# Keeping the turned w1 in DRAM between layer 1's and layer 0's backward MLP

## The chip, the cores and the metric

The kernel runs on one core of a Trainium2 chip. The metric is the device time of one execution in microseconds (us); of several runs the median counts. The core has five engines with an instruction queue each: TensorE (PE) for matrix products and transposes, VectorE (DVE), ScalarE (ACT), GpSimd (POOL) and SyncE (SP), and 16 DMA engines which move data between DRAM and the core's on-chip memory. In this kernel SyncE issues all loads and GpSimd issues all stores.

## The reference

The program computes two layers of attention over a long cache and an MLP, for one new position of two sequences, and then the gradients of the output with respect to every input but one bias.

```python
x = A_x                                        # (2, 1, 1024)
x = x + attention(layernorm(x), k_cache, v_cache, wq, wo)   # 32 query heads, 4 kv heads, 16384 keys of 128
x = x + mlp(layernorm(x), w1, b1, w2, b2)      # layernorm again, w1 (1024, 3584), gelu, w2 (3584, 1024)
x = x + attention(layernorm(x), ...)           # the same caches and weights: layer 1
x = x + mlp(layernorm(x), ...)
out_0 = x
out_1 ... out_9 = vjp(grad_out)                # A_x, k_cache, v_cache, wq, wo, w1, b1, w2, b2
```

Both layers use the same weights and the same caches. The gradients of the caches (out_2, out_3) are as large as the caches and are the sum over the two layers. All data are bf16.

## The kernel before

One pass over the program runs four phases on one core: forward layer 0 (`fwd0`), forward layer 1 (`fwd1`), backward layer 1 (`bwd1`) and backward layer 0 (`bwd0`). Between them stand the MLPs: after each `attn_fwd` the forward MLP of that layer, ahead of each `attn_bwd` the backward MLP of that layer. The place between `fwd1` and `bwd1`, where layer 1's MLP is run forward and backward, is called the turn here; the place between `bwd1` and `bwd0`, where layer 0's MLP is run backward, the middle.

The work is a list of small pieces, in the order in which they are given to `emit`; `Program.run` goes through it once, and every engine gets its instructions in that order. A piece names the chunks that it uses. A chunk is up to 1 MB of on-chip memory (128 partitions x 4096 bf16). `run` gives chunks to buffers ("slots") in the order of their first use, as early as a slot is free, and issues a chunk's load at once when it gets its slot. So the order of the loads on SyncE is the order of first use, each load waits on SyncE for the last reader of its slot, and loads run ahead of PE as far as there are slots: 14 of their own, three in the tile `last`, and two each in the tiles `e1` and `ds1` at times. From `bwd0` on six of the 14 and `last` serve other purposes. A chunk without a load (`P.chunk()`) gets a slot in the same order.

PE contracts over partitions, so for a product with a weight matrix the other way round the matrix has to be turned first, by eight 128 x 128 transposes at a time into a PSUM bank (`tp0`, `tp1`) and a copy from there by ScalarE or VectorE (`copy_bf` gives it to the less loaded one). `turned` is such a piece, which writes the turned blocks into a chunk; `w1_turned` makes the four pieces (8 + 8 + 8 + 4 transposes) that turn one of the eight chunks of w1 (128 rows x 3584). w1 is needed turned twice: by `w1_bwd(1, ...)` at the turn and by `w1_bwd(0, ...)` in the middle, and the kernel before turns it both times, from a fresh load in the middle.

At the turn the pieces for chunks 0 to 2 (`w1_now`) stand in the tail of `attn_fwd` (steps 130 to 134) and between the steps of the layernorm (`chain(lambda: mlp_in(1, xA1), ...)`), those for chunks 3 to 7 behind each chunk's forward products in `w1_fwd`. The layernorm ends in a power on GpSimd (line 463), and w1_fwd's matmuls (line 690) need its result.

In the middle the order was: the last wq products of `attn_bwd` (line 836), w1's first chunk turned as the `fill` of the layernorm's backward (`attn_in_bwd`, whose sum over partitions is the matmul of line 395), `col_to_row` for out_0 (line 418: eight fp32 transposes, two copies and the store on GpSimd), then `w2_use(i)` for the seven chunks of w2 (line 1257), with w1's chunks 1 to 5 turned between them and 6 and 7 after them, and then `w1_bwd` (line 727), behind which the turning of wo for `bwd0` begins (line 365 again).

`attn_bwd` goes through 128 steps, each with eight transposes of the V cache (line 324), their products (line 940) and, 13 steps later, the products with the K cache (line 921). `extra` hangs further pieces on steps; before, these are the last w2 products of the forward pass (`w2_last`, which finish `xM1`, the program's output, at step 118) and the turning of w2.

`PAD` sizes a tile that is never used, and so where the tiles behind it lie in memory.

Of the kernel before, what the change touches and what calls it, by code (L numbers as in the profile page):

```python
# [8 lines left out]
BF16 = mybir.dt.bfloat16  # L9
# [14 lines left out]
LAG_B = 13  # L24
LAG_K = 15
NSTG = 12
PAD = 192
STG_FROM = (0, 0, 0, 4, 8, 12)


# [23 lines left out]
class Program:  # L54
# [11 lines left out]
    def emit(self, fn, uses=()):  # L66
        i = len(self.ops)
        self.ops.append((fn, tuple(uses)))
        for c in uses:
            if c.first is None:  # L70
                c.first = i
            c.last = i
# [31 lines left out]
def kernel(  # L104
# [24 lines left out]
    nc = tc.nc  # L129
    V = nc.vector  # L130
    S = nc.scalar
    PE = nc.tensor
    GP = nc.gpsimd
# [4 lines left out]
    F = B_w1.shape[1]  # L138
    assert (B, D, HKV, SK, DH, HQ, F) == (2, 1024, 4, 16384, 128, 32, 3584)
    R = HQ // HKV  # L140
    DJ = D // 128
# [8 lines left out]
    P = Program()  # L150
    emit = P.emit
# [8 lines left out]
    small = ctx.enter_context(tc.tile_pool(name="small", bufs=3))  # L160
# [3 lines left out]
    dram = ctx.enter_context(tc.tile_pool(name="dram", bufs=1, space=bass.MemoryType.DRAM))  # L164
# [6 lines left out]
    def flat(t):  # L171
        return t.rearrange("p a b -> p (a b)")
# [5 lines left out]
    def ob():  # L178
        st["ob"] += 1
        return obanks[st["ob"] % 3]  # L180
# [29 lines left out]
    ident = const.tile([128, 128], BF16, name="ident")  # L210
    make_identity(nc, ident[:])
    identf = const.tile([128, 128], F32, name="identf")
# [11 lines left out]
    sel8 = const.tile([16, 8, 128], BF16, name="sel8")  # L224

    const.tile([128, PAD // 4], F32, name="pad")
    ident_d = dram.tile([128, 128], BF16, name="ident_d")


# [11 lines left out]
    up = [b * HKV + k for k in range(HKV) for b in range(2)]  # L241
    down = up[::-1]
# [35 lines left out]
    saved = {}  # L278
# [15 lines left out]
    def ld_rows(W, j0, rb, c0, n):  # L294

        return P.chunk(lambda ap: nc.sync.dma_start(
            ap[:, 0:rb * n].rearrange("p (j n) -> p j n", j=rb),
            W[j0 * 128:(j0 + rb) * 128, c0:c0 + n].rearrange("(j p) n -> p j n", p=128)))
# [7 lines left out]
    def ld_w1():  # L306
        return [ld_rows(B_w1, j, 1, 0, F) for j in range(DJ)]
# [4 lines left out]
    def col(c, j, n, o):  # L312
        return c.ap[:, j * n + o * 128:j * n + (o + 1) * 128]
# [19 lines left out]
    def turns_ahead(c):  # L333

        holds = [{} for _ in range(SKEW)]
        pieces = [(turn_of(lambda i=i: [c.ap[:, (i * 8 + j) * 128:(i * 8 + j + 1) * 128] for j in range(8)], h), [c])
                  for i, h in enumerate(holds)]
        return pieces, (c, holds)
# [17 lines left out]
    def turned(tiles, uses, dst, part, act=True):  # L356


        def f():
            ts = tiles()  # L360
            n = len(ts)
            st["tp"] += 1
            tp = tpb[st["tp"] % 2][:].bitcast(BF16).rearrange("p (a b) -> p a b", b=128)
            for j, t in enumerate(ts):
                PE.transpose(tp[:, j, :], t, ident[:])  # L365
            kT = dst.ap[:, part * 1024:part * 1024 + n * 128]
            if act:
                S.copy(out=kT.bitcast(I32), in_=flat(tp[:, 0:n, :]).bitcast(I32))
                load_of("act", 0.13 + 0.46 * n / 8)
            else:  # L370
                copy_bf(kT, flat(tp[:, 0:n, :]), 0.13 + 0.46 * n / 8, 0.12 + 0.57 * n / 8)
        return f, [c for c in uses if c is not dst] + [dst]
# [35 lines left out]
        emit(f, [c])  # L408

    def col_to_row(colT, dram_out):  # L410
        c = P.chunk()

        def f():
            row = c.ap[0:2, 0:D]
            for j0 in range(0, DJ, 4):
                ps = ob()[0:2, :].rearrange("p (a b) -> p a b", a=4)
                for j in range(4):
                    PE.transpose(ps[:, j, :], colT[:, j0 + j, :], identf[:])
                V.tensor_copy(out=row[:, j0 * 128:(j0 + 4) * 128], in_=flat(ps))
            GP.dma_start(dram_out, row)  # L420

        emit(f, [c])

    def chain(gen, gaps, fill=()):


        hold = {}
        fill = list(fill)

        def begin():  # L430
            hold["g"] = gen()
            next(hold["g"])

        emit(begin)
        for i in range(gaps):
            n = -(-len(fill) // (gaps - i))
            for f in fill[:n]:
                emit(*f)
            fill = fill[n:]
            emit(lambda: next(hold["g"], None))  # L440
# [242 lines left out]
    def w1_fwd(l, ws, then=lambda j: ()):  # L683

        hps = half[0, 0][:, 0:FJ * 2].rearrange("p (j b) -> p j b", b=2)
        emit(lambda: V.memset(hps, 0.0))
        for j in range(DJ):
            def f(j=j):
                for o in range(FJ):
                    PE.matmul(hps[:, o, :], lhsT=col(ws[j], 0, F, o), rhs=m_all[:, j, 2 * l:2 * l + 2],  # L690
                              start=False, stop=True, skip_group_check=True)
            emit(f, [ws[j]])
            for p in then(j):
                emit(*p)
        return hps

    def w1_turned(ws, j, dst, act=True):
        res = []
        for part, o0 in enumerate(range(0, FJ, 8)):
            n = min(8, FJ - o0)  # L700
            res.append(turned(lambda o0=o0, n=n: [col(ws[j], 0, F, o0 + o) for o in range(n)], [ws[j]], dst, part, act))
        return res

    def w2_fwd_piece(l, ws, i, fps):
        def f():
            for j in range(4):
                for o in range(DJ):
                    PE.matmul(fps[:, o, :], lhsT=col(ws[i], j, 1024, o), rhs=h_all[:, 4 * i + j, 2 * l:2 * l + 2],
                              start=False, stop=True, skip_group_check=True)
        return f, [ws[i]]  # L710
# [60 lines left out]
    def mlp_in(l, xT):  # L771
        y, rstd = yield from ln_fwd(xT[:], f"m{l}", twice=True)
        V.tensor_copy(out=m_all[:, :, 2 * l:2 * l + 2], in_=y[:])
        saved[f"m{l}"] = (y, rstd)
# [367 lines left out]
    def kept(keep, src, nm):  # L1142
        def get(g, c):
            key = (nm, g, c)
            ch = cache.pop(key, None) or ld_kv(src, g, c)
            if key in keep:
                cache[key] = ch
            return ch
        return get
# [19 lines left out]
    xM0 = vec.tile([128, DJ, 2], F32, name="xM0")  # L1169
# [8 lines left out]
    chunk_k1, chunk_v1 = kept(set(), Kv, "K"), kept(keep1, Vv, "V")  # L1178
    k_now, k_first = turns_ahead(chunk_k1(down[0], 0))
# [3 lines left out]

    ws1 = ld_w1()
    w1T = [P.chunk() for _ in range(3)] + ws1[3:]
    w1_now = [p for j in range(3) for p in w1_turned(ws1, j, w1T[j], act=False)]
    xA1 = attn_fwd(1, down, lambda: xM0, chunk_k1, chunk_v1, k_first, {130 + i: [w1_now[i]] for i in range(5)})
    chain(lambda: mlp_in(1, xA1), 2, w1_now[5:])
    hps1 = w1_fwd(1, ws1, lambda j: w1_turned(ws1, j, w1T[j], act=False) if j >= 3 else ())

    def turn_round():
        gelu_fwd(1, hps1)
# [15 lines left out]
    def chunk_v(g, c):  # L1208
        return cache.pop(("V", g, c), None) or ld_kv(Vv, g, c)

    v_now, v_first = turns_ahead(chunk_v(up[0], 0))
# [7 lines left out]
    xM1 = vec.tile([128, DJ, 2], F32, name="xM1")  # L1219
    ws2c = ld_w2()  # L1220
    extra = {}
# [15 lines left out]
    for j, s_ in enumerate(turn_steps):  # L1237
        i = j // 4
        extra.setdefault(s_, [])
        if j % 4 == 0:  # L1240
            extra[s_].append(w2_last(i))
        extra[s_].append(turned(lambda j=j, i=i: [col(ws2c[i], j % 4, 1024, o) for o in range(DJ)], [ws2c[i]],
                                ws2c[i], j % 4, act=False))
    ws1c = ld_w1()
    attn_bwd(1, up, saved["g3"], chunk_v, v_first, extra=extra, fill=w1_turned(ws1c, 0, ws1c[0]))
    col_to_row(xM1, out_0.rearrange("b s d -> (b s) d"))


    g2 = saved["gA1"]
# [2 lines left out]
    def w2_use(i):  # L1252
        def f():
            for j in range(4 * i, 4 * i + 4):
                kT = as_tiles(ws2c[i], j % 4)
                for o in range(DJ):
                    PE.matmul(dhps0[:, j, :], lhsT=kT[:, o, :], rhs=gM_all[:, o, 0:2], start=(o == 0),
                              stop=(o == DJ - 1))
        return f, [ws2c[i]]

    for i in range(FJ // 4):
        emit(*w2_use(i))
        for p in w1_turned(ws1c, i, ws1c[i], act=False) if 1 <= i < 6 else ():
            emit(*p)
    emit(lambda: V.tensor_tensor(out=dh_all[:, :, 0:2], in0=slopes[0][:], in1=dhps0, op=ALU.mult))
    for j in (6, 7):
        for p in w1_turned(ws1c, j, ws1c[j], act=False):
            emit(*p)
    dmps0 = w1_bwd(0, ws1c)
    saved["g1"] = vec.tile([128, DJ, 2], F32, name="g1")  # L1270

# [35 lines left out]
    def outputs(s, ask):  # L1307
# [6 lines left out]
        while bg and state["credit"] >= 1:  # L1314
# [3 lines left out]
        return res  # L1318

    attn_bwd(0, down, saved["g1"], chunk_v, v_first0, outputs=outputs,  # L1320
             after=lambda: col_to_row(saved["gA0"], out_1.rearrange("b s d -> (b s) d")))

    slots = [Slot(t[:], until=marks[f"bwd0 {STG_FROM[i]}"] if i < len(STG_FROM) else None) for i, t in enumerate(slot_tiles)]
    slots += [Slot(last_t[:, i * CH:(i + 1) * CH], until=marks["bwd0 0"]) for i in range(3)]
# [35 lines left out]
```

## Time and profile before

| what | value |
|---|---|
| median of 3 runs | 1188.06 us (1185.49 to 1197.34) |
| the profiled execution | 1194.48 us, its span on the core 1192.7 us |
| PE, VectorE, ScalarE, GpSimd busy | 87%, 51%, 47%, 10% of the span |
| mean granted TensorE clock | 0.864 |
| DMA | 453.83 MB, 381 GB/s over the span |
| of that loads (SyncE's queue) | 352.36 MB |
| of that stores (GpSimd's queue) | 98.66 MB |

The page and the views of the trace give the time of each instruction by line of the kernel, engine and tile. "L365 PE MATMUL tp<-ident,slot x8" is eight matmuls of line 365 (transposes are matmuls with the identity) that read a slot and write a PSUM bank. Slots carry no numbers in these names. "idle before <-X" says that the engine stood still ahead of the instruction and that X ended the wait. The granted clock is the share of full speed that TensorE had. PEld is the loading of weights into TensorE, which overlaps PE.

### The profile page before, as it was taken

The page shows a single profiled execution, that of the slowest core. Times are in us where ns is not written, and L with a number is a line of the kernel's source. Part 1 is how long each engine was busy: PE and PEld are TensorE (multiplying, and loading weights), DVE is VectorE, ACT ScalarE, POOL GpSimd, SP SyncE. Part 2 cuts the span into 40 slices and gives each one's busy share as a digit, 9 for nine tenths or more (in the row PEclk, how much of TensorE's full clock was granted, in tenths as well). Part 3 has the DMA queues.
Part 4 walks back from the last instruction along what each step waited for, and adds up shares of the span by engine and source line. Part 5 has one row for each costly group of instructions (what it writes and reads, how often), then busy time and mean ns, then how long its engine had stood idle before and what let it go on. Part 6 is the DMA issues. An engine that isn't in the chain of part 4 may idle for free. (4 is left out here: it accounts for less than half of the span.)

```text
span 1192.7 us, 44045 instructions
## 1 busy us (share of the span) xinstructions
PE 1032.3 (87%) x19762; PEld 859.1 (72%) x19805; DVE 605.4 (51%) x1266; ACT 554.8 (47%) x996; POOL 125.1 (10%) x214
## 2 busy tenths in 40 slices
PE   6878887689988988888889988988997998899996
PEld 6778786688988987888888886655565555555663
DVE  2423242224333333333434435877886787677775
ACT  2423241124333423333444424766775776567774
POOL 1000000000000000000000010322222222222222
PEclk9966695679787758889999997999998999899998
DMA  9999999989999996999999976899999999999994
GB/s 365 420 421 421 422 420 421 386 298 378 420 420 420 422 409 264 378 414 418 417 402 330 365 295 232 323 376 373 417 417 373 384 417 410 371 362 409 416 415 200
DMA packets 106041, 453.83 MB, mean 381 GB/s; under 512 B 8658, under 2 KB 8658, under 8 KB 75516
## 3 DMA queue, kind: packets, MB, share of 16 engines
q1 hardware_dynamic: 78780, 352.36, 74.5%
q0 software_dynamic: 27072, 98.66, 20.5%
q8 instruction: 154, 2.52, 0.8%
q14 instruction: 35, 0.29, 0.1%
HBM read 352.37 MB, written 98.62 MB: 378 GB/s over the span
## 5 line engine op out<-in xcount | busy, mean ns | idle before, releaser
L192 ACT COPY kT<-tp 128x512 int32<-128x512 int32 x427 | 250.0, 586 | 418.3 <-PE tp L324 391.0
L324 PE MATMUL tp<-ident,slot 128*128 128x128 bf16 x4224 | 369.2, 238 | 12.1 <-issue 5.1
L324 PEld LDWEIGHTS <-slot 128*128 128x128 bf16 x4224 | 284.4, 107 | 30.0 <-issue 12.3
L195 DVE COPY kT<-tp 128x1024 bf16<-128x1024 bf16 x209 | 144.5, 691 | 296.6 <-PE tp L324 240.8
L200 ACT CAST slot<-sc 128x512 bf16<-128x512 f32 x271 | 157.6, 589 | 50.2 <-PE sc L1072 19.6
L203 DVE CAST slot<-sc 128x512 bf16<-128x512 f32 x227 | 154.4, 688 | 38.1 <-PE sc L1025 18.6
L1025 PE MATMUL sc<-last 128*128 128x512 bf16 x324 | 119.7, 389 | 17.1 <-ACT slot L200 5.3
L921 PEld LDWEIGHTS <-slot 128*128 128x128 bf16 x1888 | 80.0, 98 | 42.5 <-issue 18.6
L940 PEld LDWEIGHTS <-kT 128*128 128x128 bf16 x2048 | 80.7, 97 | 38.5 <-issue 21.4
L1032 POOL DMA_DIRECT2D out_dram<-slot x128 | 69.0, 539 | 281.2 <-ACT slot L200 173.9
L203 DVE CAST slot<-sb 128x512 bf16<-128x512 f32 x126 | 86.7, 688 | 18.1 <-PE sb L1025 6.4
L664 PE MATMUL sc<-qd,kT 128*128 128x8 bf16 x2048 | 90.3, 171 | 2.6 <-issue 2.6
L940 PE MATMUL sc<-qd,kT 128*128 128x8 bf16 x2048 | 90.0, 170 | 1.7 <-issue 1.6
L200 ACT CAST slot<-sb 128x512 bf16<-128x512 f32 x128 | 75.3, 589 | 29.1 <-PE sb L1072 16.0
L664 PEld LDWEIGHTS <-kT 128*128 128x128 bf16 x2048 | 73.1, 99 | 3.0 <-issue 2.9
L1025 PE MATMUL sb<-last 128*128 128x512 bf16 x161 | 62.1, 386 | 6.6 <-ACT slot L200 1.6
L365 PE MATMUL tp<-ident,slot 128*128 128x128 bf16 x692 | 58.0, 239 | 6.2 <-issue 2.2
L647 PE MATMUL sb<-e,slot 128*128 128x8 bf16 x1280 | 56.7, 176 | 6.3 <-ACT e L583 3.8
L1072 PE MATMUL sc<-last 128*128 128x512 bf16 x155 | 56.6, 384 | 4.8 <-DVE last L1060 3.3
L647 PEld LDWEIGHTS <-slot 128*128 128x128 bf16 x1280 | 50.1, 102 | 9.6 <-issue 7.1
L365 PEld LDWEIGHTS <-slot 128*128 128x128 bf16 x692 | 48.2, 107 | 11.5 <-issue 9.0
L192 ACT COPY slot<-tp 128x512 int32<-128x512 int32 (+1 forms) x52 | 29.7, 574 | 52.9 <-PE tp L365 49.8
(292 smaller groups left out, 1258.7 us busy)
## 6 DMA issues: line engine op xcount, KB each, us to landing
slot<-in_A_k_cache_dram SPq DMA_DIRECT2D x101, 1024.0 KB, 10.2
slot<-in_A_v_cache_dram SPq DMA_DIRECT2D x91, 1024.0 KB, 12.1
out_dram<-slot POOLq DMA_DIRECT2D x182, 512.0 KB, 10.3
slot<-in_A_wq_dram SPq DMA_DIRECT2D x28, 1024.0 KB, 10.7
slot<-in_A_wo_dram SPq DMA_DIRECT2D x23, 1024.0 KB, 15.2
last<-in_A_v_cache_dram SPq DMA_DIRECT2D x16, 1024.0 KB, 14.4
slot<-in_B_w_dram SPq DMA_DIRECT2D x18, 896.0 KB, 13.7
slot<-in_B_w_dram SPq DMA_DIRECT2D x12, 1024.0 KB, 12.5
```

The source lines that it names most:

```text
L192: S.copy(out=dst.bitcast(I32), in_=src.bitcast(I32))
L195: V.tensor_copy(out=dst, in_=src)
L200: S.copy(out=dst, in_=src)
L203: V.tensor_copy(out=dst, in_=src)
L324: PE.transpose(tp[:, j, :], t, ident[:])
L365: PE.transpose(tp[:, j, :], t, ident[:])
L647: PE.matmul(acc, lhsT=c.ap[:, ((vi % 4) * 8 + j) * 128:((vi % 4) * 8 + j + 1) * 128], rhs=e[:, vi, :, j], start=(vi == 0 and j == 0), stop ...
L664: PE.matmul(sc[t // 64][:, :, t % 64], lhsT=kT[:, j, :], rhs=qd[:, 0, g, l, :], start=True, stop=True)
L921: PE.matmul(sb[0][:, 0:8], lhsT=c.ap[:, ((vi % 4) * 8 + j) * 128:((vi % 4) * 8 + j + 1) * 128], rhs=d[:, vi, :, j], start=(vi == 0 and j = ...
L940: PE.matmul(scb[0][t // 64][:, :, t % 64], lhsT=kT[:, j, :], rhs=qd[:, 1, g, l, :], start=True, stop=True)
L1025: PE.matmul(ps, lhsT=hold["blk"][:, 2 * (hc % 2) + u // 2, :], rhs=flat(qms[w][:, (u % 2) * 4:(u % 2) * 4 + 4, :]), start=True, stop=True)
L1032: GP.dma_start((dKv if w == 0 else dVv)[g, :, hc * 16:(hc + 1) * 16, :], stg.rearrange("p (t d) -> p t d", d=128))
```

## The change

At the turn each turned chunk of w1 is also stored into a DRAM scratch `w1_d[j]`, on GpSimd's queue (`w1_kept`). In the middle the eight chunks are loaded from there instead of from w1, and the turning of w1 in the middle goes, from the `fill` as well as from between and after `w2_use`. out_0's row is turned at step 121 of `attn_bwd(1)` instead of after it. Both output rows (out_0 and out_1) are first cast to bf16, turned by eight bf16 transposes into one bank and copied once, instead of two times four fp32 transposes and two copies. The small tile for the cast takes 32 bytes of each partition, and `PAD` shrinks by as much.

```diff
-PAD = 192
+PAD = 160
...
+    w1_d = [dram.tile([128, F], BF16, name=f"w1_d{j}") for j in range(DJ)]
     ident_d = dram.tile([128, 128], BF16, name="ident_d")
...
     def col_to_row(colT, dram_out):
+
         c = P.chunk()

         def f():
             row = c.ap[0:2, 0:D]
-            for j0 in range(0, DJ, 4):
-                ps = ob()[0:2, :].rearrange("p (a b) -> p a b", a=4)
-                for j in range(4):
-                    PE.transpose(ps[:, j, :], colT[:, j0 + j, :], identf[:])
-                V.tensor_copy(out=row[:, j0 * 128:(j0 + 4) * 128], in_=flat(ps))
+            cb = small.tile([128, DJ, 2], BF16, name="out_bf", bufs=1)
+            V.tensor_copy(out=cb[:], in_=colT[:])
+            ps = ob().bitcast(BF16)[0:2, :].rearrange("p (a b) -> p a b", a=DJ)
+            for j in range(DJ):
+                PE.transpose(ps[:, j, :], cb[:, j, :], ident[:])
+            V.tensor_copy(out=row, in_=flat(ps))
             GP.dma_start(dram_out, row)

-        emit(f, [c])
+        return f, [c]
...
+    def w1_kept(ws, j, dst):
+
+        return w1_turned(ws, j, dst, act=False) + [(lambda: GP.dma_start(w1_d[j][:], dst.ap[:, 0:F]), [dst])]
...
-    w1_now = [p for j in range(3) for p in w1_turned(ws1, j, w1T[j], act=False)]
-    xA1 = attn_fwd(1, down, lambda: xM0, chunk_k1, chunk_v1, k_first, {130 + i: [w1_now[i]] for i in range(5)})
-    chain(lambda: mlp_in(1, xA1), 2, w1_now[5:])
-    hps1 = w1_fwd(1, ws1, lambda j: w1_turned(ws1, j, w1T[j], act=False) if j >= 3 else ())
+    w1_now = [p for j in range(3) for p in w1_kept(ws1, j, w1T[j])]
+    w1_tail = {130: w1_now[0:1], 131: w1_now[1:2], 132: w1_now[2:3], 133: w1_now[3:5], 134: w1_now[5:6]}
+    xA1 = attn_fwd(1, down, lambda: xM0, chunk_k1, chunk_v1, k_first, w1_tail)
+    chain(lambda: mlp_in(1, xA1), 2, w1_now[6:])
+    hps1 = w1_fwd(1, ws1, lambda j: w1_kept(ws1, j, w1T[j]) if j >= 3 else ())
...
-    ws1c = ld_w1()
-    attn_bwd(1, up, saved["g3"], chunk_v, v_first, extra=extra, fill=w1_turned(ws1c, 0, ws1c[0]))
-    col_to_row(xM1, out_0.rearrange("b s d -> (b s) d"))
+    extra.setdefault(121, []).append(col_to_row(xM1, out_0.rearrange("b s d -> (b s) d")))
+    ws1c = [P.chunk(lambda ap, j=j: nc.sync.dma_start(ap[:, 0:F], w1_d[j][:])) for j in range(DJ)]
+    attn_bwd(1, up, saved["g3"], chunk_v, v_first, extra=extra)
...
     for i in range(FJ // 4):
         emit(*w2_use(i))
-        for p in w1_turned(ws1c, i, ws1c[i], act=False) if 1 <= i < 6 else ():
-            emit(*p)
     emit(lambda: V.tensor_tensor(out=dh_all[:, :, 0:2], in0=slopes[0][:], in1=dhps0, op=ALU.mult))
-    for j in (6, 7):
-        for p in w1_turned(ws1c, j, ws1c[j], act=False):
-            emit(*p)
     dmps0 = w1_bwd(0, ws1c)
...
-             after=lambda: col_to_row(saved["gA0"], out_1.rearrange("b s d -> (b s) d")))
+             after=lambda: emit(*col_to_row(saved["gA0"], out_1.rearrange("b s d -> (b s) d"))))
```

## The prediction

> **What bounds the kernel now.** I read the page's head first, then busy time by stage, then the waits, then the two places that the change touches in order of time.
>
> The page's head, with the busy share of the DMA engines in 40 slices:
>
> ```profile
> span 1192.7 us, 44045 instructions
> ...
> DMA  9999999989999996999999976899999999999994
> ```
>
> The DMA engines look like the bound, with holes only at the layer-1 turn (slice 15) and between the two backward passes. The windows by stage say which engine sets the pace in each; columns are window and length, busy time of PE, its weight loads, VectorE, ScalarE and GpSimd, granted clock, DMA share and GB/s.
>
> ```profile
> core 0: us, PE busy (x) PEld busy (x) DVE busy (x) ACT busy (x) POOL busy (x), PEclk, DMA share, GB/s
> 425.00:450.00 25.00, 21.39 (x464) 19.84 (x462) 7.16 (x23) 6.28 (x13) 0.69 (x1) 0.62 1.02 406
> 450.00:465.00 15.00, 12.98 (x322) 12.04 (x321) 6.56 (x21) 6.32 (x12) 0.00 (x0) 0.98 0.30 111
> 465.00:490.00 25.00, 21.10 (x422) 20.56 (x420) 8.86 (x34) 7.03 (x13) 0.00 (x0) 0.67 1.01 419
> 510.00:610.00 100.00, 84.76 (x2069) 83.31 (x2069) 38.56 (x94) 38.63 (x66) 0.00 (x0) 0.91 1.02 419
> 610.00:682.00 72.00, 67.53 (x1725) 65.13 (x1726) 30.02 (x67) 31.31 (x54) 0.00 (x0) 1.00 0.95 354
> 682.00:715.30 33.30, 29.59 (x683) 27.53 (x681) 11.82 (x29) 9.33 (x17) 4.54 (x3) 0.87 0.80 307
> 740.00:830.00 90.00, 80.31 (x1061) 51.58 (x1061) 71.38 (x122) 64.06 (x119) 25.42 (x42) 0.98 0.93 351
> 830.00:1170.00 340.00, 308.73 (x4296) 200.53 (x4319) 261.13 (x457) 234.76 (x430) 84.78 (x147) 0.96 1.00 397
> ```
>
> At the turn (450 to 465) the engines move 111 GB/s against 419 when full, so some 308 x 15 = 4.6 MB of room lies unused there. From 610 on the rate is below full and PE is busy 89 to 94% of each stage: PE's order is the pace.
>
> Who waits for loads. Of PE's waits from 421 us to the end, one is put to a DMA:
>
> ```profile
> PE sb L647 <- DMA last<-in_B_w_dram: 0.5, 1, 0.5
> ```
>
> SyncE, which issues the loads, from 421 to 690 us (waited for; total, times, longest):
>
> ```profile
> SPq L291 <- PE tp L324: 80.4, 26, 5.4
> ...
> SPq L291 <- PE sb L727: 20.5, 7, 18.9
> ...
> SPq L296 <- DMA out_dram<-last: 10.5, 1, 10.5
> ```
>
> PE lost 0.5 us to late data in 766 us, while SyncE waited for PE to free buffers (18.9 us in one piece for w1_bwd, L727, which is the hole). Even where DMA is full after the turn, loads run ahead of their use. A saved microsecond of PE order between 682 and 715 should therefore reach the end; added DMA bytes should not, unless they exceed the lead.
>
> **The change, part by part.**
>
> *Removed between the backward passes.* PE in order of time (start, length, line, count):
>
> ```profile
> 681.44 0.54 PE L836 MATMUL sc<-dq_all,slot 128*128 128x2 bf16 x16
> ...
> 684.36 0.53 PE L395 MATMUL sb<-lb_s,onesf 128*128 128x4 f32 x2
> 684.75 1.76 PE L418 MATMUL sc<-identf,xM 128*2 128x128 f32 x8
> 686.40 1.75 PE L1257 MATMUL sc<-gM_all,slot 128*128 128x2 bf16 x64
> ...
> 708.66 0.85 PE L727 MATMUL sb<-dh_all,last 128*128 128x2 bf16 x28
> ...
> 715.25 3.60 PE L365 MATMUL tp<-ident,slot 128*128 128x128 bf16 x32
> ```
>
> ```profile
> 681.00:709.00 28.00, 17.24 (x224) 14.68 (x224) 0.88 0.78 303
> ```
>
> The second fence is line 365 alone: the 224 transposes that turn w1 hold PE for 17.24 us, and PE's waits for their evictions lie between them. They go, with 32 copies on ScalarE and VectorE, and so do the eight float transposes of L418; the layernorm's matmul (L395) even stood behind the first 28 of them. What they covered comes into the open. The old stretch ran from 681.98 (end of L836) to 715.25, 33.3 us. The new one has four links. First, the layernorm's chain. The same chain stands uncovered at the end of the program:
>
> ```profile
> 1170.38 0.34 PE L836 MATMUL sb<-dq_all,slot 128*128 128x2 bf16 x8
> ...
> 1173.27 1.01 PE L418 MATMUL sc<-identf,gA 128*2 128x128 f32 x4 [1.30 <-DVE gA L968]
> ...
> 1174.08 1.06 PE L418 MATMUL sb<-identf,gA 128*2 128x128 f32 x4
> ...
> 1176.85 1.01 PE L1057 MATMUL sc<-ident,dq_all 128*4 128x128 bf16 x8
> 1177.97 0.70 DVE L1060 COPY last<-sc 4x1024 bf16<-4x1024 bf16 x1 [0.75 <-PE sc L1057]
> ```
>
> From 1170.72 to 1173.27 is 2.55 us; with one more cast, 2.8. Second and fourth, w2_use and w1_bwd, 224 two-column matmuls each, now back to back. Their rate, from L727 alone (busy PE, count, PE's weight loads, clock):
>
> ```profile
> 462.00:464.40 2.40, 2.40 (x96) 2.40 (x96) 1.00 0.25 51
> 464.90:468.00 3.10, 3.08 (x116) 2.99 (x113) 0.50 1.03 425
> ```
>
> That is 25 ns at full clock and 26.6 ns at half, so a clock that falls here costs little; 224 x 26 = 5.8, twice. Third, the slope product on VectorE, formerly behind the last transposes: about 0.5 us by the links of the chain above. Sum 2.8 + 5.8 + 0.5 + 5.8 = 14.9; saved 33.3 - 14.9 = 18.4, call it 18.2. Bounds: nothing, if read-back data come too late (a rival), to 33.3 - 11.6 = 21.7 with both chains covered.
>
> *The read-back* loads the same 8 x 896 KB in SyncE's old places, but SyncE now reaches them differently. out_0's row, formerly stored after the pass, takes a buffer from the K loads at about 641 us and holds it to its store, now at step 121, near 662. One K load then waits for that store, and the eight w1 loads queue behind it. The old issues in SyncE's order of time, and the row's store from its issue to landing (shortest, median, longest of two):
>
> ```profile
> 659.22 2.98 SPq L291 DMA_DIRECT2D slot<-in_A_k_cache_dram  x2
> 666.11 0.33 SPq L296 DMA_DIRECT2D last<-in_B_w_dram  x1
> 669.97 11.51 SPq L296 DMA_DIRECT2D slot<-in_B_w_dram  x7
> ```
>
> ```profile
> DMA to landing us min/median/max: 1.6/3.3/5.1
> ```
>
> ```profile
> 678.76 1.20 PE L921 MATMUL sb<-ds,slot 128*128 128x8 bf16 x40
> ```
>
> Transposed near 662.5, copied 0.7, the row is issued at 664 and lands by 669; the K load follows at 669 instead of 662. The last 32 of those 40 matmuls at 679 are its first use. At 419 GB/s it and the eight w1 loads (8.4 MB) are through 20 us later, about 691 to 693 with latency. w1_bwd, from 691.1, needs the last chunk near 696, and the two wo loads behind it (2.5 us each) meet their first uses 2 to 3 us early. I take no wait, with a bound of 7 us for the K load's whole delay.
>
> *The row itself* at step 121 sits in PE's order inside the PE-bound stage: eight bf16 transposes (1.01 us for eight at the reduced clock, above; half of that at full) and a wait for the cast: +0.7. At the end, two fp32 groups (1173.27 to 1175.14, 1.87 us) become a cast plus eight bf16 transposes, about 1.3: -0.6.
>
> *Added at the turn.* Eight stores of 128 x 3584 bf16, 7.34 MB, on GpSimd's queue. Two of them, j = 1 and 2, stand ahead of the layernorm's power on that queue, for which VectorE, and after it PE's first w1_fwd matmul, wait:
>
> ```profile
> 439.41 0.43 DVE L195 COPY slot<-tp 128x512 bf16<-128x512 bf16 x1 [0.47 <-PE tp L365]
> ...
> 439.98 0.69 POOL L463 TENSOR_TENSOR m_rstd<-ln_vpe,neghalf 128x2 f32<-128x2 f32 x1 [177.76 <-DVE ln_vpe L460]
> ...
> 441.25 0.89 PE L690 MATMUL sc<-m_all,slot 128*128 128x2 bf16 x28 [1.71 <-DVE sc L686]
> ```
>
> ```profile
> L1032 POOL DMA_DIRECT2D out_dram<-slot x128: 531/532/570, 740.5 to 1183.6; - x128
> ...
> DMA to landing us min/median/max: 2.9/10.3/18.0
> ```
>
> The last copy of j = 2 ends at 439.84; an issue of 0.53 us follows, so the power starts about 0.5 late: +0.5 (0.5 to 1.5, if seven-KB rows issue slower). The other six stores have nothing behind them on GpSimd until out_0. The seven loads that take w1's buffers after w1_bwd (462 to 468) now also wait for landings; issued from about 427 to 456 for the first seven, the stores land by 466 at the median, 474 at the longest.
>
> The bytes: 7.34 MB less the 4.6 MB of the hole is 2.7 MB, 6.5 us of lag for loads issued after 463. Taken as nothing: the DMA engines already stood nearly still for longer than that (450 to 465) and PE met no late load afterwards. If that cover were gone, the price is 7.34 / 0.419 = 17.5 us. Those are the bounds, 0 and 17.5.
>
> The Trainium skill, "DMA: Bandwidth & Descriptors", section "Queues, rings and completion order", says each DMA engine takes turns between its queues packet by packet, so a store would take half the rate from the w1 loads that w1_fwd wants next. No run here shows two queues at the turn yet. By that page's fabric ceiling (435 GB/s, "Specifications") the stores would cost an estimated 16.9 us if nothing hid them.
>
> *Sum:* -18.2 + 0.7 - 0.6 + 0.5 = -17.6 us. On the profiled execution's own 1194.48 us that is 1176.9; it ran 6.4 above the median of the runs shown, 1188.06, which becomes **1170.5**. The last stage keeps its own order, buffers and load distance, so I let it start earlier as a whole.
>
> **Rivals.**
>
> *A, stores paid in full.* The eight stores delay the w1 loads, and through them the turn's chain, by their whole 17.5 us; the middle still gains. 1188.1 - 17.6 + 17.5 = 1188. For it: 406 GB/s at 425 to 450, already full. Against: the hole, and PE's single DMA wait.
>
> *B, the read-back is late.* SyncE stands at the K load until out_0's row has landed; w1, wo and v come 7 us late in a stage where I counted 2 to 3 us of room, then another 2 or so behind a fuller queue. The gain falls by about 7: 1177.5. For it: SyncE already lost 10.5 us to this row. Against: its landing takes at most 5.1.
>
> *C, slower: bytes are the bound.* The last pass runs at DMA share 1.00 for 340 us. If it ends when its bytes are through rather than when PE is, an earlier start gives nothing, and the stores' 17.5 us are added: 1205.6. It decides from the point where PE begins to wait for loads or its staging for stores. For it: that share. Against: 397 GB/s there and 351 before it, against 419; PE busy 91%.
>
> **How the numbers follow.** Forecast 0.64, A 0.16, B 0.12, C 0.08. From 1164, nearly the largest saving of the middle (21.7) and the sum's smaller terms with a little run-to-run spread, to 1189, which takes in A and B; C lies outside. A measurement of this kernel can tell about 1% from no change: 11.9 us. The forecast and a small part of B lie beyond: faster 0.65; most of B and A are the same, 0.24; C and a piece of A slower, 0.11.
>
> **What would show it.** Right: line 365 absent between the passes, w1_bwd ending 14 to 16 us after the last wq matmul, a second DMA queue with 7.3 MB filling the hole, no new PE wait on loads. A: w1_fwd of layer 1 waiting for DMA and the turn longer by several microseconds. B: PE idle on DMA at w1_bwd or at the wo transposes. C: waits on out_dram growing after 830 while the last pass stretches. Wrong altogether if the stretch from L836 to w1_bwd's end stays near 33 us.

## The result, and the profile after

The changed kernel took 1184.8 us (median of 20 runs, 1179.4 to 1191.8); the kernel before, run beside it, 1195.5 (20 runs). The ratio is 0.9934, 95% interval 0.9912 to 0.9956; two later repetitions gave 0.9888 [0.9848, 0.9929] and 0.9894 [0.9858, 0.9931]. The change is faster, by about 11 us in medians and by 8 to 13 us by the three ratios, where 17.6 were forecast. The three runs of before that the prediction started from (1188.06) were quick ones, but that concerns only the absolute time, not the saving. The profiled executions went from 1194.48 to 1184.97 us, a difference of 9.5.

The head of the page after:

```profile
span 1183.2 us, 43570 instructions
## 1 busy us (share of the span) xinstructions
PE 1013.8 (86%) x19538; PEld 843.3 (71%) x19581; DVE 596.1 (50%) x1251; ACT 545.4 (46%) x979; POOL 129.8 (11%) x222
...
DMA  9999999989999999999998997899999999999994
...
q0 software_dynamic: 28224, 106.00, 22.2%
q8 instruction: 153, 2.51, 0.8%
```

The hole in slice 15 is gone, and so are 224 matmuls. Queue q0 (GpSimd's stores) carries 106.00 MB. The row that turned out to matter is the last: a queue of 153 packets of kind "instruction", 16 KB each (2.51 MB / 153).

The windows by stage after, in the columns of the prediction's:

```profile
425.00:450.00 25.00, 20.53 (x444) 19.18 (x442) 6.26 (x23) 6.09 (x12) 2.95 (x5) 0.61 1.02 416
450.00:465.00 15.00, 12.86 (x299) 11.85 (x299) 7.18 (x22) 6.40 (x13) 2.12 (x4) 1.00 1.02 418
465.00:490.00 25.00, 20.57 (x428) 20.02 (x426) 8.36 (x33) 6.27 (x11) 0.00 (x0) 0.66 1.02 425
...
652.40:686.70 34.30, 31.36 (x780) 30.03 (x776) 14.77 (x38) 14.05 (x24) 0.54 (x1) 0.95 0.92 356
686.70:689.50 2.80, 0.63 (x5) 0.56 (x4) 1.75 (x12) 0.00 (x0) 0.00 (x0) 0.54 1.05 439
689.50:698.60 9.10, 6.24 (x224) 6.10 (x224) 0.00 (x0) 0.00 (x0) 3.97 (x2) 0.50 1.02 407
698.90:707.10 8.20, 6.27 (x226) 6.19 (x226) 0.00 (x0) 0.00 (x0) 0.00 (x0) 0.50 1.04 422
```

The turn now moves 418 GB/s where it moved 111. In the middle w2_use took 9.1 us and w1_bwd 8.2, and in both PE worked for only 6.3. What it waited for in between stands in the timeline of PE (start, length, line, count; in brackets the idle time before and what ended it):

```profile
686.37 0.34 PE L844 MATMUL sb<-dq_all,slot 128*128 128x2 bf16 x8
687.37 0.59 PE L397 MATMUL sc<-lb_s,onesf 128*128 128x4 f32 x2 [0.66 <-DVE lb_s L477]
689.47 3.55 PE L1266 MATMUL sc<-gM_all,slot 128*128 128x2 bf16 x128 [1.51 <-DVE gM_all L978]
...
693.74 1.60 PE L1266 MATMUL sc<-gM_all,slot 128*128 128x2 bf16 x55
698.18 0.40 PE L1266 MATMUL sc<-gM_all,slot 128*128 128x2 bf16 x9 [2.84 <-issue]
698.88 0.88 PE L735 MATMUL sb<-dh_all,last 128*128 128x2 bf16 x28 [0.30 <-DVE dh_all L1272]
699.63 2.56 PE L735 MATMUL sb<-dh_all,slot 128*128 128x2 bf16 x91
704.12 2.21 PE L735 MATMUL sb<-dh_all,slot 128*128 128x2 bf16 x77 [1.93 <-issue]
706.20 0.89 PE L735 MATMUL sb<-dh_all,last 128*128 128x2 bf16 x28
706.94 2.64 PE L367 MATMUL tp<-ident,slot 128*128 128x128 bf16 x23
710.06 2.90 PE L367 MATMUL tp<-ident,slot 128*128 128x128 bf16 x33 [0.48 <-issue]
```

PE stops three times for "issue", that is for nothing which the profile shows: 2.84, 1.93 and 0.48 us. Count the matmuls between the stops: 9 + 28 + 91 = 128, and 77 + 28 + 23 = 128. The stops come 5.94 us apart and fall inside a chunk (119 is four chunks of 28 and seven more), so no chunk's landing ends them. The read-back was there anyway: SyncE issued its last load at 684.6, and the rows of that line say

```profile
DMA to landing us min/median/max: 7.7/9.4/10.5
```

so all of it had landed by about 695, ahead of w1_bwd's start at 698.88.

This is theory F, on which the experiments turn: PE's own instructions arrive by DMA in blocks. 19538 matmuls and 19581 weight loads are 39119 instructions; over 153 packets that is 256 per packet, so a packet holds 128 pairs of weight load and matmul. The number of packets follows that of the pairs: among the experiments below, 152 in e3, which has 112 pairs fewer, and 173 in e4, which has 2560 more (20 packets of 128). The trace's records of this queue put one packet into or just ahead of each stop: they start at 695.76, 701.77 and 707.68, last 0.9 us, and PE goes on 1.4 to 1.5 us after the end of each, at 698.18, 704.12 and 710.06. With the 16 DMA engines full, as here, a packet arrives only about every 5.9 us, 46 ns per pair. The Trainium skill ("Trainium Architecture — The Big Picture", section "The software stack") gives 64 bytes per instruction, with which 16 KB is the same 256; that section speaks of the streams being moved when the program is loaded, whereas this trace has 153 such packets within the execution.

Where the time went, in us, from one profile of before and three of the changed kernel. The pass runs from layer 1's first product on V to its last wq product, the middle from there to layer 0's first product on V; the first row includes the forward half, which scatters by some microseconds from run to run:

| stretch | before | after | repeats | difference | forecast |
|---|---|---|---|---|---|
| start to the pass | 480.54 | 481.69 | 481.94, 484.26 | +1.2, +1.4, +3.7 | +0.5 |
| the pass | 201.44 | 205.02 | 205.06, 203.69 | +3.6, +3.6, +2.3 | +0.7 |
| the middle | 54.98 | 41.76 | 41.66, 42.48 | -13.2, -13.3, -12.5 | -18.2 |
| last pass and tail | 455.75 | 454.70 | 455.68, 455.76 | -1.1, -0.1, 0.0 | -0.6 |

### The profile page after: what moved, and what is told of

Its sections match the earlier page's. It is cut to its first block, busy times and chain, and to the rows that moved or that the text cites. A ratio compares the mean times of both kernels' runs of the same rounds, so it can differ in the third digit from the quotient of the medians.

```text
span 1183.2 us, 43570 instructions
## 1 busy us (share of the span) xinstructions
PE 1013.8 (86%) x19538; PEld 843.3 (71%) x19581; DVE 596.1 (50%) x1251; ACT 545.4 (46%) x979; POOL 129.8 (11%) x222
## 3 DMA queue, kind: packets, MB, share of 16 engines
q0 software_dynamic: 28224, 106.00, 22.2%
q8 instruction: 153, 2.51, 0.8%
## 5 line engine op out<-in xcount | busy, mean ns | idle before, releaser
L326 PE MATMUL tp<-ident,slot 128*128 128x128 bf16 x4224 | 369.1, 238 | 9.9 <-issue 3.9
L326 PEld LDWEIGHTS <-slot 128*128 128x128 bf16 x4224 | 284.3, 107 | 27.5 <-issue 10.3
L200 ACT CAST slot<-sc 128x512 bf16<-128x512 f32 x263 | 153.0, 588 | 60.7 <-PE sc L1080 29.9
L203 DVE CAST slot<-sc 128x512 bf16<-128x512 f32 x242 | 163.7, 688 | 33.4 <-PE sc L1033 15.0
L1033 PE MATMUL sc<-last 128*128 128x512 bf16 x325 | 117.3, 386 | 17.5 <-DVE last L1068 5.6
L929 PEld LDWEIGHTS <-slot 128*128 128x128 bf16 x1888 | 80.6, 98 | 44.9 <-issue 20.8
L200 ACT CAST slot<-sb 128x512 bf16<-128x512 f32 x136 | 80.1, 589 | 17.7 <-PE sb L1033 9.0
L203 DVE CAST slot<-sb 128x512 bf16<-128x512 f32 x111 | 76.4, 688 | 21.2 <-PE sb L1033 8.0
L651 PEld LDWEIGHTS <-slot 128*128 128x128 bf16 x1280 | 50.3, 102 | 10.5 <-issue 6.9
L367 PE MATMUL tp<-ident,slot 128*128 128x128 bf16 x528 | 47.6, 246 | 5.4 <-issue 3.9
L929 PE MATMUL sb<-ds,slot 128*128 128x8 bf16 x864 | 41.4, 176 | 11.0 <-issue 11.0
L1033 PEld LDWEIGHTS <-last 128*128 128x128 bf16 x512 | 38.4, 98 | 16.7 <-issue 8.4
```

Of the source, the lines that this page charges most:

```text
L200: S.copy(out=dst, in_=src)
L203: V.tensor_copy(out=dst, in_=src)
L651: PE.matmul(acc, lhsT=c.ap[:, ((vi % 4) * 8 + j) * 128:((vi % 4) * 8 + j + 1) * 128], rhs=e[:, vi, :, j], start=(vi == 0 and j == 0), stop ...
L929: PE.matmul(sb[0][:, 0:8], lhsT=c.ap[:, ((vi % 4) * 8 + j) * 128:((vi % 4) * 8 + j + 1) * 128], rhs=d[:, vi, :, j], start=(vi == 0 and j = ...
L1033: PE.matmul(ps, lhsT=hold["blk"][:, 2 * (hc % 2) + u // 2, :], rhs=flat(qms[w][:, (u % 2) * 4:(u % 2) * 4 + 4, :]), start=True, stop=True)
```

## Experiments

Three theories are named in the expectations. F is the one above. S says that the missing microseconds are the price of the eight stores. D gathers the rivals in which something else sets the rate of the middle's matmuls: the arrival of the data, or the halved clock. R comes later, for the row of out_0.

### e1: the stores alone

The kernel before, with `w1_kept` at the turn and everything else as it was:

```diff
-    w1_now = [p for j in range(3) for p in w1_turned(ws1, j, w1T[j], act=False)]
+    w1_now = [p for j in range(3) for p in w1_kept(ws1, j, w1T[j])]
...
-    hps1 = w1_fwd(1, ws1, lambda j: w1_turned(ws1, j, w1T[j], act=False) if j >= 3 else ())
+    hps1 = w1_fwd(1, ws1, lambda j: w1_kept(ws1, j, w1T[j]) if j >= 3 else ())
```

> The kernel before with the eight stores of the turned w1 at the turn, and nothing else; the middle turns w1 again. Theory F (PE's instructions arrive too slowly in the middle): the stores are nearly free, layer 1's first product step of the backward pass comes 0.5 to 1.5 us later than before, and the whole is 0 to 2 us slower. Theory S (the stores' bytes or their place on GpSimd's queue eat the missing gain): 7 us or more slower than before, with waits on DMA at the turn or a bwd1 pass stretched by that much. Theory D (the read-back comes late) says the same as F here.

Measured: 1198.85 us (10 runs) against 1196.15, ratio 1.0022 [0.9988, 1.0057], so between 1.4 us gained and 6.8 lost. The windows at the turn:

```profile
450.00:465.00 15.00, 12.71 (x291) 11.59 (x289) 7.30 (x22) 6.70 (x13) 2.12 (x4) 1.00 1.03 420
```

The hole takes the stores (420 GB/s). They most likely cost about 3 us, far from the 17.5 of rival A. Layer 1's first product on V came 2.0 us later (482.53 against 480.54), a little more than the 0.5 to 1.5 expected.

### e2: the changed kernel without the stores

The read-back is replaced by loads of w1 as it stands, so layer 0's w1_bwd multiplies unturned blocks.

```diff
-        return w1_turned(ws, j, dst, act=False) + [(lambda: GP.dma_start(w1_d[j][:], dst.ap[:, 0:F]), [dst])]
+        return w1_turned(ws, j, dst, act=False) + [(lambda: None, [dst])]
...
-    ws1c = [P.chunk(lambda ap, j=j: nc.sync.dma_start(ap[:, 0:F], w1_d[j][:])) for j in range(DJ)]
+    ws1c = ld_w1()
```

> The changed kernel without the eight stores; the middle loads w1 itself, of the same bytes, and does not turn it, so its products are of the wrong matrix and only its time counts. F: the middle, from the last wq product to the end of w1_bwd, stays at 20 us (20.4 in the changed kernel), the turn gets about 1 us back, the whole is 9 to 12 us faster than before. S: the missing gain returns, 16 us or more faster than before. D: the middle stays near 20 us if late loads set it, as the loads stay.

Measured: 1186.32 us (4 runs), ratio 0.9883 [0.9824, 0.9943], an interval that takes in the changed kernel's three ratios. The middle keeps its length, 41.1 us, and its two stops (2.37 and 1.93 us). What is missing there is not the stores' price: S falls for the middle. The pass, however, took 200.9 us here against 203.7 to 205.1 with stores, though its last part, from step 112 on, was no shorter (34.5 us; 34.3 with stores). The part on the bytes at the end comes back to this.

### e3: half of layer 0's w1_bwd left out

```diff
+        no = FJ if l == 1 else FJ // 2
...
-                for o in range(FJ):
+                for o in range(no):
```

> The changed kernel with 14 instead of 28 products per chunk in layer 0's w1_bwd (half of the sum is left out); all loads stay. 112 pairs of weight load and matmul fewer. F, at 46 ns a pair: the middle falls from 20.4 us to about 15.2. By the forecast's 25 ns a pair: to 17.6. D: w1_bwd still ends with the landing of the last chunk or the wo behind it, so the start of the wo transposes moves by less than 1 us.

Measured, one run: 1178.53 us. The stretch from the last wq product to the end of w1_bwd, which the expectation calls the middle, fell from 20.4 to 15.1 us, as F had it, and so the transposes of wo start 5 us earlier, counted from that product, where D had less than 1. The whole middle up to layer 0's first product on V, however, fell only from 41.8 to 38.3 us, so there the 112 pairs were worth 3.4 us, 31 ns each. The timeline of PE shows the reason:

```profile
695.53 0.40 PE L1267 MATMUL sc<-gM_all,slot 128*128 128x2 bf16 x9 [2.66 <-issue]
696.23 0.51 PE L735 MATMUL sb<-dh_all,last 128*128 128x2 bf16 x14 [0.30 <-DVE dh_all L1273]
696.60 2.38 PE L735 MATMUL sb<-dh_all,slot 128*128 128x2 bf16 x84
698.84 0.51 PE L735 MATMUL sb<-dh_all,last 128*128 128x2 bf16 x14
699.22 0.91 PE L367 MATMUL tp<-ident,slot 128*128 128x128 bf16 x7
702.02 2.24 PE L367 MATMUL tp<-ident,slot 128*128 128x128 bf16 x19 [1.89 <-issue]
```

w1_bwd itself now runs without a stop, 3.1 us for 112, and the stop has moved into the transposes behind it, nearly as long (1.89 us) as it was. That the stop keeps its place in the instruction count (9 + 14 + 84 + 14 + 7 = 128) and not its place in the work speaks for F. So F's 46 ns are right for the stretch and too much for the whole middle, where the price lies nearer to the 25 ns of PE's own pace, probably because only part of it is held up by the blocks; one profile can't say more.

### e4: the same pairs, with quiet and with full DMA engines

Behind the end of the changed kernel stand 1536 pairs of a 128 x 128 weight load and a two-column matmul with nothing else running, then 1024 pairs while SyncE loads 32 chunks of 1 MB:

```diff
+        for n in range(1536):
+            PE.matmul(half[0, 0][:, 0:2], lhsT=t[:, 0:128], rhs=gM_all[:, 0, 0:2], start=True, stop=True)
...
+        for n in range(32):
+            nc.sync.dma_start(slot_tiles[6 + n % 8][:].rearrange("p (t d) -> p t d", d=128), Kv[n % 8, :, 0:32, :])
+        for n in range(1024):
+            PE.matmul(half[0, 0][:, 0:2], lhsT=Et[0][:, 0:128], rhs=gM_all[:, 0, 0:2], start=True, stop=True)
```

> The changed kernel with a probe behind its end, outside the reference's work: 1536 pairs of weight load and two-column matmul with no load in flight (only the last stores), then 1024 more while 32 loads of 1 MB run. F: about 26 ns a pair in the quiet part beyond the first stores (a 16-KB block of instructions every 3.4 us or faster), 46 ns a pair under load (a block every 5.9 us), so 40 and 47 us. If blocks take 5.9 us whatever the DMA engines do: 46 ns in both. If the matmuls themselves are slower in a long run (clock at half): the same figure in both, and no idle time of PE between them.

The timeline of PE, first in the quiet part, then in the loaded one:

```profile
1202.06 3.57 PE L1330 MATMUL sc<-gM_all,slot 128*128 128x2 bf16 x128 [0.17 <-issue]
1205.80 3.58 PE L1330 MATMUL sc<-gM_all,slot 128*128 128x2 bf16 x128 [0.17 <-issue]
...
1239.97 3.57 PE L1336 MATMUL sc<-gM_all,e 128*128 128x2 bf16 x128 [2.92 <-issue]
1246.18 3.57 PE L1336 MATMUL sc<-gM_all,e 128*128 128x2 bf16 x128 [2.64 <-issue]
1252.12 3.57 PE L1336 MATMUL sc<-gM_all,e 128*128 128x2 bf16 x128 [2.37 <-issue]
```

The windows of the same two parts (clock, DMA share and GB/s are the last three columns):

```profile
1180.00:1210.00 30.00, 28.43 (x1033) 27.94 (x1031) 0.00 (x0) 0.00 (x0) 0.00 (x0) 0.50 0.02 4
1222.00:1262.00 40.00, 24.34 (x877) 23.76 (x874) 0.00 (x0) 0.00 (x0) 0.00 (x0) 0.50 1.01 424
```

The groups have 128 matmuls in both parts and take 3.57 us in both. At an idle DMA the next group starts 0.17 us later (3.7 us per block, 29 ns per pair), at 424 GB/s 2.4 to 2.9 us later (5.9 to 6.2 us per block, 46 to 49 ns per pair). In all, the 1536 quiet pairs took 44.5 us, where F expected 40, and the 1024 loaded ones 46.8, where it expected 47. The records of the instruction queue show where the time goes: a packet starts 1.1 us after PE starts a block in the quiet part, but 3.6 to 3.9 us after it in the loaded part, when PE has just run dry; once started, it takes about 1 us in either. The clock is 0.50 in both, so it is not the clock, and the loaded part's operands lie still in a tile that no load writes, so it is not the data. D falls, and F is shown in isolation.

### e5 and e6: the row of out_0

The pass is 2 to 4 us longer, its last 34 us among them (31.9 before from step 112 on, 34.3 after), and SyncE's timeline after shows the wait that the prediction described:

```profile
663.98 0.33 SPq L293 DMA_DIRECT2D slot<-in_A_k_cache_dram  x1
671.48 0.33 SPq L293 DMA_DIRECT2D last<-in_A_k_cache_dram  x1
671.90 0.38 SPq L1254 DMA_DIRECT2D last<-w_d  x1
```

Theory R blames the row. e5 keeps the cast at step 121, puts the transposes into the layernorm's gap behind the pass, and takes the row's place from spare columns of two w1 chunks, so no load waits for it; e6 puts the whole row behind the pass, as before.

```diff
-    extra.setdefault(121, []).append(col_to_row(xM1, out_0.rearrange("b s d -> (b s) d")))
...
+    extra.setdefault(121, []).append((row_cast, ()))
...
-    attn_bwd(1, up, saved["g3"], chunk_v, v_first, extra=extra)
+    attn_bwd(1, up, saved["g3"], chunk_v, v_first, extra=extra, fill=[(row_store, ws1c[0:2])])
```

```diff
-    extra.setdefault(121, []).append(col_to_row(xM1, out_0.rearrange("b s d -> (b s) d")))
...
+    emit(*col_to_row(xM1, out_0.rearrange("b s d -> (b s) d")))
```

> The changed kernel again, beside the next kernels on the same chip. Both theories: ratio to the kernel before 0.990 to 0.996, middle stretch (last wq product of layer 1 to first wo product of layer 0) about 41.8 us as in its first profile.

> The cast of the first output stays at step 121, but its eight transposes run in the gap of the layernorm behind attn_bwd(1), and its store reads from columns of two w1 chunks that nothing else uses, so it holds no slot of the chunk pool and no later load waits for it. Theory R (the row, not the instruction supply, is what lengthened the end of layer 1's pass from 31.9 to 34.3 us between step 112 and its last product: SyncE's K load waited for the store): that stretch comes back to 32.0 to 32.8, and the kernel is 1.5 to 2.5 us faster than the changed kernel. Theory F (TensorE's instructions arrive 128 pairs at a time, some 46 ns a pair while the DMA engines are full, and the end of the pass runs against that): moving eight pairs wins at most 8 x 46 ns = 0.4 us and the stretch stays at 34; the difference to the changed kernel is within 0.5 us.

> The changed kernel with the first output's bf16 row put back behind attn_bwd(1), as it stood before; stores and read-back kept. Theory R: step 112 to the last product of the pass is 32.0 to 32.8 us instead of 34.3, and the row behind costs its 8 transposes and a copy on the path, about 1 us, so 0.5 to 1.5 us faster than the changed kernel. Theory F: the pass stays at about 34, and the row behind adds up to 1 us: 0 to 1 us slower than the changed kernel.

Measured: the changed kernel again 1186.21 us (the ratio is above), e5 1187.14, ratio 0.9904 [0.9869, 0.9940], e6 1189.76, ratio 0.9938 [0.9910, 0.9966]. SyncE's timeline of e5 shows that its wait is gone:

```profile
661.78 2.83 SPq L293 DMA_DIRECT2D slot<-in_A_k_cache_dram  x2
669.07 2.78 SPq L1270 DMA_DIRECT2D last<-w_d  x2
```

Yet e5's pass took 205.9 us, 34.9 of it from step 112 on: no gain, and R falls. In e6 these were 205.6 and 33.7, so the row costs the pass nothing that one profile can show, while behind the pass it lengthens the middle from 41.7 to 44.2 us. By these single profiles the move of the row is worth some 2.5 us. The medians put e6 3.5 us behind the changed kernel beside it, with intervals that overlap; R had expected it faster, F at most 1 us slower.

### e7: less read back

Only 512 of each chunk's 3584 columns are read back (the rest of what w1_bwd multiplies is what the buffer held).

```diff
-    ws1c = [P.chunk(lambda ap, j=j: nc.sync.dma_start(ap[:, 0:F], w1_d[j][:])) for j in range(DJ)]
+    ws1c = [P.chunk(lambda ap, j=j: nc.sync.dma_start(ap[:, 0:512], w1_d[j][:, 0:512])) for j in range(DJ)]
```

> The changed kernel with only 512 of the 3584 columns of each w1 chunk read back (so layer 0's w1_bwd multiplies stale columns): 6.3 MB less through the DMA engines ahead of and in the middle, the same 455 pairs on TensorE. Theory F: where the DMA share falls well below 1 in the middle, blocks of 128 pairs come 3.4 to 4.5 us apart instead of 5.9, w2_use and w1_bwd take 6 to 7 us each instead of 9.1 and 8.2, and the end is 4 us earlier or more. If instead the half clock of TensorE or the loads themselves set the middle's rate (theory D), w2_use and w1_bwd stay at 8 to 9 us each. If other loads fill the freed DMA time (share stays at 1.0), this run tells nothing between them.

Measured, one run: 1180.76 us. The windows of its end of the pass and of its middle:

```profile
652.90:685.10 32.20, 30.26 (x779) 28.77 (x776) 14.79 (x38) 14.07 (x24) 0.53 (x1) 1.00 0.75 269
687.80:696.10 8.30, 6.27 (x224) 6.13 (x224) 0.00 (x0) 0.00 (x0) 3.95 (x2) 0.50 1.02 372
696.40:702.50 6.10, 6.10 (x226) 6.10 (x226) 0.00 (x0) 0.00 (x0) 0.00 (x0) 0.50 0.94 339
```

Where the share fell below 1, PE lost its stop: w1_bwd took 6.1 us of which PE worked 6.1, and the end of the pass 32.2 us instead of 34.3. Part of the stop only moved: among the transposes behind w1_bwd one of 0.92 us stands where it was 0.48. During w2_use other loads filled the room (share 1.02), and it stayed at 8.3. In e6 it was the other way round: there w2_use ran at a share of 0.65 and took 7.3 us, and w1_bwd, at 1.00, took 8.8. Same pairs, same clock (0.50): the price follows the DMA share.

### e9: loads of the last pass held back until w1_bwd is through

Eight loads of V, K and wo chunks whose first use comes after 730 are issued behind w1_bwd, by giving the first of them the buffer that w1_bwd frees last:

```diff
+                held = c is order[order.index(self.hold[0]) + 4]
+                if held and i < self.hold[1]:
+                    break
-                s = next((s for s in free if s.fits(c)), None)
+                s = next((s for s in (free[::-1] if held else free) if s.fits(c)), None)
...
     dmps0 = w1_bwd(0, ws1c)
+    P.hold = (ws1c[-1], len(P.ops))
```

> The changed kernel a third time, beside the next kernel on the same chip: ratio to the kernel before 0.989 to 0.995, middle stretch (last wq product of layer 1 to the first matmul on V of layer 0) 41.7 us.

> The changed kernel with seven or eight loads of the last pass (V, K and wo chunks, 1 MB each, issued from 692 to 706 us and first used from 732 on) held back until layer 0's w1_bwd is through, about 707: the loads only move, none is added, and TensorE's 455 pairs are the same. Theory F: the DMA engines' queue runs empty near 693 to 697 instead of staying full, the instruction blocks behind that come 3.5 to 4.5 us apart, w1_bwd falls from 8.2 to 6.0 to 6.5 us and the stall at the end of w2_use from 2.8 to 1 to 2.5; middle stretch 38 to 40 us, the kernel 1.5 to 4 us faster than the changed kernel unless the last pass then waits for the late loads. Theory D (half clock or the weight-load path sets w1_bwd's rate): w1_bwd stays at 8.2 and the kernel is equal or, by the late loads, slower.

Its windows over w2_use and w1_bwd, and PE's timeline within w1_bwd:

```profile
689.30:699.00 9.70, 6.42 (x224) 6.21 (x224) 0.00 (x0) 0.00 (x0) 3.97 (x2) 0.50 1.03 412
699.30:705.90 6.60, 6.31 (x227) 6.22 (x227) 0.00 (x0) 0.00 (x0) 0.00 (x0) 0.50 0.28 113
```

```profile
700.07 2.56 PE L738 MATMUL sb<-dh_all,slot 128*128 128x2 bf16 x91
702.91 2.21 PE L738 MATMUL sb<-dh_all,slot 128*128 128x2 bf16 x77 [0.27 <-issue]
```

The stop inside w1_bwd shrank from 1.93 to 0.27 us at the same place in the count (28 + 91 matmuls), and w1_bwd from 8.2 to 6.6, with no byte and no matmul taken out. The instruction packets start 4.4 and 3.4 us apart there (696.31, 700.69, 704.04), where they were 6.0 and 5.9 us apart. The middle is 40.35 us against 41.66 to 42.48. As a kernel it is no better: 1187.33 us, ratio 0.9920 [0.9889, 0.9951], against 1184.24 of the changed kernel beside it. F had expected it 1.5 to 4 us faster, and the stop in w2_use at 1 to 2.5 us, where it grew to 3.19. Its pass, in which nothing differs, took 207.1 us in the profile, at a granted clock of 0.90 there against 0.93 to 0.94 in the three profiles of the changed kernel; a gain of 1 to 2 us is not to be told from such spread. No version that beats the changed kernel was found.

## Why the prediction had the direction right and the size wrong

*The direction and the path held.* PE's order did set the end: layer 0's pass began 8.5 us earlier in the first profile and the kernel ended 9.5 earlier. Line 365's transposes are gone from the middle, the stores went into the hole, and no load was late on PE. That the time measured, 1184.8, still lies between the bounds of 1164 and 1189 is luck: the upper one was drawn to take in rivals A and B, and neither came about.

*The step that failed is the rate of w2_use and w1_bwd* ("back to back", 224 x 26 ns = 5.8, twice). The other links were right: the layernorm's chain took 2.76 us (686.71 to 689.47; forecast 2.8) and the slope product 0.3 (forecast 0.5). The two products took 9.1 and 8.2, and w1_bwd ended 20.4 us after the last wq product (19.6 and 20.4 in the repetitions), where the prediction's own sign of being right was 14 to 16. Of the 5.7 us too much, 4.8 are the two stops for instructions and 0.9 the rate itself, 28 ns rather than 26. My rate came from two windows, of 96 and 116 matmuls, in the turn's w1_bwd, whose 224 matmuls ran without a stop. One of the windows was even full (1.03, 425 GB/s), which seemed to settle the point. But the stop stands in the profile before, eleven transposes behind that run:

```profile
467.84 1.33 PE L365 MATMUL tp<-ident,slot 128*128 128x128 bf16 x11
470.26 2.42 PE L365 MATMUL tp<-ident,slot 128*128 128x128 bf16 x21 [1.09 <-issue]
```

So the run was over before PE had used up what it held, and the change put two such runs in a row. The old middle showed little of the limit (one stop of 0.70 us within w1_bwd) because its 683 matmuls were spread over 33.3 us by evictions, 49 ns each, just slower than 46. Taking out transposes gained until PE met the supply: 450 pairs x 46 ns = 20.7 us, near the 19.6 to 20.4 measured from the last wq product to the end of w1_bwd. The prediction's own table had a row for this: 2069 matmuls in 100 us between 510 and 610, 48 ns each at full DMA share. And of PE's waits it counted only those on loads, 0.5 us; the waits between 500 and 610 us of the same profile begin (total, times, longest) with

```profile
PE sb L921 <- issue: 10.0, 8, 2.2
```

and over the whole pass PE waited 16.3 us for "issue" before the change.

*The row at step 121 and SyncE.* The order of events was as told (the K load issued at 671.48 where I had 669), and "I take no wait" held: PE's waits name no load there, and e5, which takes SyncE's wait away, gained nothing. In e6, without the row, the whole pass is no shorter (205.6 us) and its last part by 0.6 (33.7 against 34.3): that would fit the term +0.7, but one profile does not show it.

*The bytes, "taken as nothing".* This is the second term that was too small. The pass became 2.3 to 3.6 us longer in the three profiles of the changed kernel, against 0.7 forecast, and 2.1 longer in e1, with the stores alone; it was 0.5 shorter in the one without stores and 0.5 longer in the one with a short read-back. So as a whole it goes with the bytes. No load came late, as predicted, but PE's waits for "issue" within the pass rose from 16.3 us to 17.5 to 19.1, which is half to three quarters of what it grew by. That the bytes slow the instruction blocks fits this. But the end of the pass was as long without the stores (e2), and single profiles scatter by 1 to 2 us, so the cause is argued and not shown.

*The turn*, forecast +0.5 for the power behind the store on GpSimd. Its timeline:

```profile
440.27 0.53 POOL L710 DMA_DIRECT2D w_d<-slot  x1 [3.22 <-issue]
440.82 0.72 POOL L467 TENSOR_TENSOR m_rstd<-ln_vpe,neghalf 128x2 f32<-128x2 f32 x1
```

The power starts at 440.82 instead of 439.98, 0.84 late, directly behind the store: the mechanism was right, the size within its bounds.

*The tail*, forecast -0.6, stayed the same: from the last wq product (ending at 1161.23) to the end of the span are 21.9 us, against 22.0 before. PE did save 0.5 us up to its first product behind the row (4.1 us after the last wq product instead of 4.6), but the end of the span did not follow.

*The rivals.* A: e1 bounds the stores' price by 6.8 us, where A wanted 17.5. B: SyncE did wait for the row's store (7.1 us), but w1 was in place before its use. C: the last pass, at a DMA share of 1.00, took 454.7 to 455.8 us against 455.8, and so started earlier as a whole.

## What to carry to other kernels

A rate read from a burst may be a rate from stock: before multiplying it, count the instructions in the burst, and ask what refills the engine while the DMA engines are full. Short matmuls that are freed of their waits while the DMA engines are full ran here not at their own pace but at that of the instruction queue; so look for "issue" stops at equal distances in the count, and price the pairs that stay at the pace of a long full stretch (here 46 to 48 ns), not at the length of their row. What a removed pair gains can be less: 31 ns in e3. Moving loads away from such a burst shortens the burst, as e9 showed, but whether the kernel gains depends on who carries the load instead.

## What the runs showed of the hardware

PE's instructions came in packets of 16 KB, 256 instructions, on a DMA queue of their own, during the execution. With idle DMA engines a block followed the one before in 3.7 us, just behind PE's own 3.57 for 128 two-column pairs; with the engines at 424 GB/s it took 5.9 to 6.2 us. The packets were 0.8% of the DMA time, so in these stretches a queue with hardly any bytes set the pace of the busiest engine. The clock was granted at 0.50 during both, and a pair took 28 ns in either.
